# Turns by TensorE through one PSUM tile, a longer convolution lead, later units and loads of two blocks

## The chip, the cores and the metric

One core of one Trainium2 chip. The metric is device time in microseconds (us) of one execution; the kernel before and each variant were run alternately on the same chip, and fast runs are compared with fast runs (a single-core run over 1.5% above the fastest of its kernel counts as slow and is left out of the ratios). The runs e9 and e10 are from another chip than e1 to e8; each ratio is against the kernel before on the chip of the run.

## The reference, cut to what matters

```python
# x (8, 4224, 192); weight (8 heads, 7 taps); d_inner = 512
w = softmax(weight, axis=-1)
out = einsum('hk,bskhg->bshg', w, windows_of_7(x_padded))        # causal convolution
proj = out @ w_in; val, gate = proj[..., :512], proj[..., 512:]
for t in range(S):
    h = a[0, 0] * h + val[:, t, :]; ys[:, t, :] = h                # scan, from 0 in each sequence
result = (silu(gate) * ys) @ w_out
```

## The kernel before

The 33,792 rows of all sequences are cut into blocks of 960. Each engine has one part of the work: TensorE convolves, projects and multiplies by `w_out`; VectorE scans; ScalarE does SiLU and empties PSUM; GpSimd multiplies SiLU and scan and issues the loads of `x` (which cast to bf16). The order on every engine is the order in the program. Four words recur: a *pair* is one pass of the main loop (two steps), a *piece* half a block's convolution, a *turn* brings a convolved block into columns, and a *unit* is the last multiplication for 512 rows; the prediction begins with them in full. The parts that the change touches:

```python
    # P = 128, NC = 4, M = 120, BT = 8, BANK = 512, XG = 4; tiles of PSUM: 2 of values, 2 of all else
    xb_pool = ctx.enter_context(tc.tile_pool(name="xb", bufs=3))
    # ...
    ps_v = ctx.enter_context(tc.tile_pool(name="ps_v", bufs=2, space=bass.MemoryType.PSUM))
    ps_m = ctx.enter_context(tc.tile_pool(name="ps_m", bufs=2, space=bass.MemoryType.PSUM))

    def vtile():
        return ps_v.tile([P, 2 * BANK], FP32, name="pv")

    def mtile():
        return ps_m.tile([P, 2 * BANK], FP32, name="pm")

    def xtile(b):
        g, k = divmod(b, XG)
        if g not in xbs:
            xbs[g] = xb_pool.tile([K, XG * BT, D], BF16, name="xb")
        return xbs[g], FIRST[b] - FIRST[g * XG]

    def rows(a, n):
        return dataclasses.replace(
            xf, offset=(a * M - HB) * D, ap=[[D, K], [M * D, n], [1, D]]
        )

    def load_cast(b0, b1):
        xt, a0 = xtile(b0)
        n = sum(SIZES[b0:b1])
        if b1 == NSB:
            n -= 1
            e = HB + LAST
            nc.gpsimd.memset(xt[:, a0 + n, :], 0.0)
            nc.gpsimd.dma_start(xt[0:e, a0 + n, :], xf[T - e : T, :])
        nc.gpsimd.dma_start(xt[:, a0 : a0 + n, :], rows(FIRST[b0], n))
    # ...
    def turn_pe(b, engs):
        nh = SIZES[b] // 2
        y = ycs.pop(b)
        xc = xctile(b)
        w = half(b)
        for r in range(3):
            pool, name = (ps_v, "pv") if b == 0 and r == 2 else (ps_m, "pm")
            pt = pool.tile([P, 4 * BANK], BF16, name=name)
            for i in range(nh):
                nc.tensor.transpose(
                    pt[:, i * M : i * M + M],
                    y[0:M, (r * nh + i) * P : (r * nh + i + 1) * P], ident,
                )
            copy(
                engs[r], cols(xc, r * nh, nh),
                pt[:, 0:w].rearrange("p (t m) -> p t m", m=M),
            )
    # ... proj(), val(), gate(): 2 matmuls each, full (128 rows) or the rest (64 rows), into pv or pm
    def out_unit(u):
        ps = mtile()
        osb = o_pool.tile([P, UB, D], FP32, name="osb")
        first = None
        for k in range(2):
            mms = out_mm(ps, u, k, range(NC))
            if first is not None:
                apart(mms, [first], "another PSUM bank of the same tile")
            first = out_copy(nc.scalar, ps, osb, k)
        nc.sync.dma_start(o4[u], osb)

    BY_PE = (0, 1, 2, 3)

    def conv_piece(b, part):
        ps = mtile()
        conv_mm(ps, b, part)
        conv_evac([(nc.scalar, (0, 2))], ps, b, part)
        if part and b not in BY_PE:
            turn(b)
    # ...
    NP = NSTEP // 2
    LEAD = 6
    early = {0: (3, 4), 1: (4, 5), 2: (5, 6), 3: (6, 8), 6: (8, 10), 9: (10, 12)}
    for p in range(NP):
        s = 2 * p
        b = s // NC
        scan(s)
        if p:
            val(s + 1, True, True)
        gate(s, True, True)
        val(s + 1, False, False)
        gate(s, False, False)
        val(s + 2, False, True)
        gate(s + 1, False, True)
        silu(s)
        mul(nc.gpsimd, s)
        gate(s + 1, True, False)
        val(s + 2, True, False)
        silu(s + 1)
        if p < NP - 1:
            scan(s + 1)
            mul(nc.gpsimd, s + 1)
        if p in early:
            load_cast(*early[p])
        if p == 1:
            nc.gpsimd.dma_start(wout, moe_w_out.rearrange("(c p) m -> p c m", p=P))
        if s % NC == 0 and b >= 6 and b % XG == 2 and b + 6 < NSB:
            load_cast(b + 6, min(b + 6 + XG, NSB))
        late = 0 if b >= NSB - 7 else 2
        if LEAD <= p < NP - 2 and done_step(u) < s - late:
            units(1)
        if p == 0:
            turn_pe(1, [nc.scalar] * 3)
        if p in (2, 4):
            turn_pe(p // 2 + 1, [nc.scalar] * 3)
        for _ in range({0: 0, 1: 2, 4: 2, 13: 2}.get(p, 1)):
            if todo:
                b1, part = todo.pop(0)
                conv_piece(b1, part)
        if p == 0:
            nc.scalar.copy(xs, xsf)
        if p == 2:
            firsts()
        if p % 2 == 0 and p // 2 + 1 < NSB:
            patch(p // 2 + 1)
```

## Time and profile before

| kernel before | |
|---|---|
| time, median of the first 3 runs (lowest, highest) | 336.76 us (335.98, 337.2) |
| span in the profile | 335.6 us |
| busy: TensorE, VectorE, GpSimd, ScalarE | 95, 92, 92, 79% |
| first scan starts, last scan ends | 12.41 us, 327.91 us |
| two pairs in the steady middle | 8.74 us |

A pair holds two scans, and a scan can run only if TensorE has finished its values. So the start times of the scans are the kernel's clock: a delay of any engine that matters shows as a gap between two scans, and all later scans are late by it. Busy shares alone would not tell where the time goes, since three engines are nearly full. The views themselves stand in the prediction.

### The profile page before, as it was taken

The numbers are of one execution on the slowest core, as the hardware profiler recorded it, in microseconds if no ns is written. First come the engines' busy times: TensorE is split into PE (matmuls) and PEld (weight loads), VectorE is DVE, ScalarE is ACT, GpSimd is POOL, SyncE is SP. The second block draws the span as 40 slices with busy tenths as digits, with TensorE's granted clock in tenths as the row PEclk, the third lists the DMA queues.
The fourth block names the chain that finished last, engine by engine and source line by source line (L and its number), as shares of the span: only waits on it lengthen the run. The fifth ranks groups of instructions, "written<-read, shape, count | busy, mean of one in ns | idle before, by whom it ended". The sixth has DMA issues, their size and how long they took to land.

```text
span 335.6 us, 6814 instructions
## 1 busy us (share of the span) xinstructions
PE 319.6 (95%) x2581; PEld 191.1 (57%) x2581; DVE 309.9 (92%) x190; ACT 263.8 (79%) x454; POOL 308.7 (92%) x198
## 2 busy tenths in 40 slices
PE   8888799999999999999999999899999999999984
PEld 3443366565666665555666666465556566555554
DVE  2798899998999998999999999999999989999991
ACT  4587888788888887888888888788888878887663
POOL 5699999999998998899999999999999999989992
PEclk9999999999999999999999999999999999999999
DMA  7669979999996799559985999399978995444223
GB/s 173 71 65 121 109 133 200 158 218 169 215 192 177 116 187 255 159 97 173 222 227 108 176 190 237 96 142 212 255 143 108 135 293 144 140 132 131 96 93 144
DMA packets 100968, 53.80 MB, mean 160 GB/s; under 512 B 91371, under 2 KB 92423, under 8 KB 100935
## 3 DMA queue, kind: packets, MB, share of 16 engines
q1 hardware_dynamic: 59943, 39.32, 52.2%
q0 software_dynamic: 40448, 13.55, 37.6%
q10 hardware_dynamic: 544, 0.49, 0.5%
q8 instruction: 20, 0.33, 0.5%
q14 instruction: 13, 0.11, 0.1%
HBM read 28.46 MB, written 25.95 MB: 162 GB/s over the span
## 4 chain that ended last, share of the span: by engine, by line
PE 77%; DMA 8%; POOL 4%; DVE 3%; issue 3%; ACT 3%; DVEq 0%; ACTq 0%; POOLq 0%
PE pm L482 23%; PE pm L409 16%; PE pv L409 14%; PE pv L415 10%; DMA xc<-yc 8%; PE pm L415 6%; PE pm L253 5%; POOL y L473 3%; DVE h L450 3%; PE pm L193 2%; ACT sg L435 1%; POOL xb L128 1%; ACT yc L102 0%; ACT xc L102 0%; PE pm L367 0%
## 5 line engine op out<-in xcount | busy, mean ns | idle before, releaser
L473 POOL TENSOR_TENSOR y<-sg,h 128x960 bf16<-128x960 bf16 (+3 forms) x159 | 280.3, 1791 | 15.7 <-ACT sg L435 15.2
L450 DVE TENSOR_TENSOR_SCAN h<-av,h,pv 128x960 bf16<-128x960 f32 (+5 forms) x140 | 265.7, 1937 | 10.3 <-issue 2.7
L435 ACT ACTIVATE sg<-pm 128x960 bf16<-128x960 f32 (+2 forms) x144 | 135.6, 953 | 44.1 <-PE pm L415 34.7
L482 PEld LDWEIGHTS <-y 128*128 128x128 bf16 x1056 | 91.1, 114 | 12.8 <-issue 0.8
L482 PE MATMUL pm<-wout,y 128*128 128x192 bf16 x1056 | 97.6, 246 | 0.4 <-ACT sg L435 0.3
L409 PEld LDWEIGHTS <-w 128*128 128x128 bf16 x576 | 48.9, 97 | 61.2 <-issue 32.4
L409 PE MATMUL pv<-xc,w 128*128 128x480 bf16 (+2 forms) x288 | 80.7, 362 | 1.8 <-DVE h L450 1.5
L409 PE MATMUL pm<-xc,w 128*128 128x480 bf16 (+2 forms) x288 | 81.3, 364 | 0.7 <-ACT yc L102 0.6
L102 ACT COPY osb<-pm 128x384 f32<-128x384 f32 x131 | 62.7, 479 | 15.0 <-PE pm L482 12.9
L102 ACT CAST yc<-pm 128x256 bf16<-128x256 f32 (+2 forms) x140 | 59.7, 490 | 1.8 <-PE pm L253 1.6
L415 PE MATMUL pv<-xc,w 64*128 64x480 bf16 (+2 forms) x288 | 53.6, 365 | 5.4 <-DVE h L450 3.4
L415 PEld LDWEIGHTS <-w 64*128 64x128 bf16 x576 | 23.1, 94 | 53.8 <-issue 39.7
L415 PE MATMUL pm<-xc,w 64*128 64x480 bf16 (+2 forms) x288 | 52.7, 358 | 0.0
L450 DVE TENSOR_TENSOR_SCAN h<-av,pv 128x720 bf16<-128x720 f32 (+4 forms) x32 | 42.5, 1331 | 1.5 <-PE pv L415 1.5
L253 PE MATMUL pm<-xb,tb 126*128 126x192 bf16 (+1 forms) x280 | 34.1, 244 | 0.9 <-ACT xc L102 0.4
L253 PEld LDWEIGHTS <-tb 126*128 126x128 bf16 x288 | 24.7, 97 | 3.0 <-issue 1.7
L128 POOL DMA_DIRECT2D xb<-in_x_dram x14 | 20.5, 1464 | 0.1
L193 PE MATMUL pm<-wm 128*128 128x512 bf16 x24 | 8.6, 522 | 1.3 <-DVE wm L138 1.3
L193 PEld LDWEIGHTS <-wm 128*128 128x128 bf16 x24 | 2.8, 126 | 5.6 <-issue 3.9
L102 ACT COPY xc<-pm 128x480 bf16<-128x480 bf16 (+1 forms) x10 | 5.2, 549 | 0.4 <-PE pm L367 0.4
L367 PE MATMUL pm<-ident,yc 120*128 120x120 bf16 x42 | 3.8, 214 | 1.6 <-ACT sg L435 1.3
L367 PEld LDWEIGHTS <-yc 120*128 120x128 bf16 x45 | 2.9, 97 | 3.4 <-issue 2.2
(58 smaller groups left out, 27.4 us busy)
## 6 DMA issues: line engine op xcount, KB each, us to landing
out_dram<-osb SPq DMA_DIRECT2D x65, 384.0 KB
xb<-in_x_dram POOLq DMA_DIRECT2D x5, 1512.0 KB, 23.0
xb<-in_x_dram POOLq DMA_DIRECT2D x3, 756.0 KB, 10.2
xb<-in_x_dram POOLq DMA_DIRECT2D x5, 378.0 KB, 5.5
xb<-in_x_dram POOLq DMA_DIRECT2D x1, 1275.8 KB, 20.9
xc<-yc SPq DMA_TRANSPOSE x32
w1r<-in_moe_w_in_dram SPq DMA_DIRECT2D x1, 448.0 KB
xr<-in_x_dram ACTq DMA_DIRECT2D x1, 283.5 KB
```

Of the source, the lines that this page charges most:

```text
L102: return eng.copy(o, i) if eng is nc.scalar else eng.tensor_copy(o, i)
L128: nc.gpsimd.dma_start(xt[:, a0 : a0 + n, :], rows(FIRST[b0], n))
L193: nc.tensor.matmul(pw[:, 0:BANK], wm[:, 0:P], wm, start=True, stop=True)
L253: nc.tensor.matmul(pc[:, :, i * G : i * G + G], tb[:, h, :], xt[:, a0 : a0 + n, h * G : h * G + G], start=True, stop=True, skip_group_chec ...
L367: nc.tensor.transpose(pt[:, i * M : i * M + M], y[0:M, (r * nh + i) * P : (r * nh + i + 1) * P], ident,)
L409: nc.tensor.matmul(o, w1[:, m], cols(xc, k * nh, nh), start=start, stop=not start, skip_group_check=True,)
L415: nc.tensor.matmul(o, w2[r, m], cols(xc, 2 * nh, nh, r), start=start, stop=not start, skip_group_check=True,)
L435: nc.scalar.activation(sg[:, 0 : 2 * w], pgs.pop(s)[:, BANK - w : BANK + w], Act.Silu)
L450: nc.vector.tensor_tensor_scan(h[:, lo:hi], av[:, c : c + 1].to_broadcast([P, hi - lo]), pv[:, BANK - w + lo : BANK - w + hi], initial=0.0 ...
L473: eng.tensor_mul(yr[c][:, ring(t0 + lo, hi - lo)], sg[:, lo:hi], h[:, lo:hi])
L482: nc.tensor.matmul(ps[:, o : o + D], yr[c][:, r.start + j : r.stop : UB], wout[:, c, :], start=(c == 0 and j % 2 == 0), stop=(c == NC - 1) ...
```

## The change

Its intent: take the waits out of the first pairs (turns through one PSUM tile, block 4 turned by TensorE as well, the first unit one pair later, one more pair between a block's convolution and its use), and replace the bursts of four-block loads, behind which DMA transposes landed late, by loads of two blocks. In passing, the load of the output weights goes from pair 1 to pair 5, and small casts from ScalarE to GpSimd. Cut to its core:

```diff
-    XG = 4                                            # blocks per tile of x
+    XG = 2
-    xb_pool = ...(name="xb", bufs=3)
+    xb_pool = ...(name="xb", bufs=6)
 # turn_pe: for b > 0 one tile for all three groups, emptied by two copies (2/3 and 1/3)
-        for r in range(3):
-            pool, name = (ps_v, "pv") if b == 0 and r == 2 else (ps_m, "pm")
+        if b == 0:
+            groups = [(ps_m, "pm", (0,)), (ps_m, "pm", (1,)), (ps_v, "pv", (2,))]
+        else:
+            groups = [(ps_m, "pm", (0, 1, 2))]
 # ... (casts of xs and ysp moved to GpSimd)
-    BY_PE = (0, 1, 2, 3)
+    BY_PE = (0, 1, 2, 3, 4)
-    LEAD = 6
-    early = {0: (3, 4), 1: (4, 5), 2: (5, 6), 3: (6, 8), 6: (8, 10), 9: (10, 12)}
+    LEAD = 7
+    TURN = {2: 2, 4: 3, 5: 4}
+    early = {0: (3, 4), 1: (4, 5), 2: (5, 6), 3: (6, 7), 4: (7, 8)}
+    later = {2 * b1 - 9: (b1, b1 + 2) for b1 in range(8, NSB, 2)}
         mul(nc.gpsimd, s)
+        if p in later:
+            load_cast(*later[p])
         gate(s + 1, True, False)
-        if p == 1:
+        if p == 5:
             nc.gpsimd.dma_start(wout, ...)
-        if s % NC == 0 and b >= 6 and b % XG == 2 and b + 6 < NSB:
-            load_cast(b + 6, min(b + 6 + XG, NSB))
-        for _ in range({0: 0, 1: 2, 4: 2, 13: 2}.get(p, 1)):     # pieces per pair
+        for _ in range({0: 0, 1: 2, 3: 2, 6: 2}.get(p, 1)):
-        if p == 2:
+        if p == 3:
             firsts()
```

## The prediction

> **Words.** A block is 960 rows of the flattened sequence (8 groups of 120), worked off in four steps (one per 128 inner channels), so two loop passes ("pairs", p) per block. A unit is the last multiplication for 512 rows (16 matmuls, L482); a piece is half a block's convolution (4 matmuls, L253). A turn brings a convolved block into columns: by TensorE (L367, then copies), or by a DMA transpose.
>
> **What bounds the kernel now.** I began with the page's busy times and its chain.
>
> ```profile
> PE 319.6 (95%) x2581; PEld 191.1 (57%) x2581; DVE 309.9 (92%) x190; ACT 263.8 (79%) x454; POOL 308.7 (92%) x198
> ...
> PE 77%; DMA 8%; POOL 4%; DVE 3%; issue 3%; ACT 3%; DVEq 0%; ACTq 0%; POOLq 0%
> ```
>
> Three engines are above 92%, so little can be won: 2% is 6.7 us. The chain is TensorE's for 77%. To see the steady pace I read the timeline of TensorE in the middle, where one unit falls into each pair.
>
> ```profile
> 176.74 1.48 PE L482 MATMUL pm<-wout,y 128*128 128x192 bf16 x16
> ...
> 181.19 1.48 PE L482 MATMUL pm<-wout,y 128*128 128x192 bf16 x16
> ...
> 185.49 1.48 PE L482 MATMUL pm<-wout,y 128*128 128x192 bf16 x16
> ```
>
> Pairs take 4.45 and 4.30 us in turn, 8.74 for two (4.37 each). TensorE's own work is 4.30; two scans of VectorE, at a pitch of 2.13 to 2.17 us, are about as much. Both lock into this cycle through the PSUM tiles of the values. The change touches nothing in it: 65 pairs at 4.37 stay. What can be won is the time lost beside the cycle, and it shows as gaps of the scans, so the timeline of VectorE was next (in brackets the idle time before, and its releaser).
>
> ```profile
> 14.77 3.20 DVE L450 TENSOR_TENSOR_SCAN h<-av,pv 128x720 bf16<-128x720 f32 x2 [0.70 <-PE pv L415]
> 18.23 1.65 DVE L450 TENSOR_TENSOR_SCAN h<-av,pv 128x720 bf16<-128x720 f32 x1 [0.27 <-PE pv L415]
> ...
> 27.51 8.53 DVE L450 TENSOR_TENSOR_SCAN h<-av,h,pv 128x960 bf16<-128x960 f32 x4 [1.30 <-PE pv L415]
> 37.46 8.53 DVE L450 TENSOR_TENSOR_SCAN h<-av,h,pv 128x960 bf16<-128x960 f32 x4 [1.42 <-POOL y L473]
> ...
> 78.13 15.46 DVE L450 TENSOR_TENSOR_SCAN h<-av,h,pv 128x960 bf16<-128x960 f32 x8 [0.85 <-POOL y L473]
> ...
> 131.60 1.11 DVE L450 TENSOR_TENSOR_SCAN h<-av,h,pv 128x432 bf16<-128x432 f32 x1 [0.52 <-issue]
> ...
> 270.56 2.21 DVE L450 TENSOR_TENSOR_SCAN h<-av,h,pv 128x960 bf16<-128x960 f32 x1 [0.44 <-PE pv L409]
> 273.34 15.46 DVE L450 TENSOR_TENSOR_SCAN h<-av,h,pv 128x960 bf16<-128x960 f32 x8 [0.56 <-PE pv L415]
> ```
>
> The gaps of 1.30 and 1.42 follow the turns of blocks 2 and 3 (pairs 2 and 4); I do not believe the label POOL of the second, for the value matmuls that the scan needs end at 37.4. The 0.85 follows the doubled piece of pair 13. Those at 131 and 270 follow late DMA transposes, which the chain in order of time shows (start, length):
>
> ```profile
> 113.01 13.86 DMA xc<-yc
> ...
> 254.61 14.32 DMA xc<-yc
> ```
>
> and the page's DMA issues name the disturber (a load of four blocks in flight for 23 us):
>
> ```profile
> xb<-in_x_dram POOLq DMA_DIRECT2D x5, 1512.0 KB, 23.0
> xb<-in_x_dram POOLq DMA_DIRECT2D x3, 756.0 KB, 10.2
> xb<-in_x_dram POOLq DMA_DIRECT2D x5, 378.0 KB, 5.5
> ```
>
> By the landings in the trace a transpose takes 3.7 us with no load in flight, 7.4 (issued at 37.29) and 9.1 (at 63.63) inside a load of two blocks, and 11 to 14.3 inside one of four.
>
> **What the skill says.** "DMA: Bandwidth & Descriptors", Issuing engines are not separate DMA queues: DMAs of all issuing engines share the 16 DMA engines and interleave. The trace agrees: 3.7 us against 11 to 14. Same page, Anatomy of one DMA: about 2.0 us plus bytes over 436 GB/s. For 378 KB that gives 2.9 us; the trace has 5.5, so I take the trace. "TensorE: Matmul & The Clock Gate", Part 4: a transpose takes 275 to 390 ns alone. The trace has 214 ns, and four in a row take 0.37 us, a pitch of 52 ns. "PSUM — Partial Sum Buffer", the four PSUM rules: GpSimd can't reach PSUM; hence the new staging tile that ScalarE fills for GpSimd.
>
> **The change, part by part.**
>
> (1) Turns with one PSUM tile. Before, 12 transposes went through three tiles out of a pool of two, so TensorE waited for both SiLUs and then for the first copy:
>
> ```profile
> 23.38 0.38 PE L367 MATMUL pm<-ident,yc 120*128 120x120 bf16 x4
> 24.20 0.82 PE L367 MATMUL pm<-ident,yc 120*128 120x120 bf16 x8 [0.44 <-ACT sg L435]
> ```
>
> Now all 12 wait only for the first SiLU and take 12 x 0.052 = 0.6 us. ScalarE copies 960 and 480 columns (by the copies of 360 and 480, 0.46 and 0.56 us, some 0.96 + 0.51 = 1.47) in place of 3 in 1.58: nothing gained there. The next gate matmul still waits for both copies. I walked pairs 0 to 7 by hand with these lengths, in the program's order on each engine:
> - pair 0: turn of block 1; scan 3 no longer waits, at 17.96 in place of 18.23.
> - pair 2: copies end at 25.2, the gate matmuls 0.5 later, the value's second half 0.4 after; scan 7 at about 26.3 (27.51 before).
> - pair 3: two pieces and the small convolution of the sequences' first rows (moved here from pair 2), whose tile waits for the first piece's copies; scan 9 at 31.0 (31.74), a new gap of 0.4.
> - pair 4: turn of block 3; scan 11 at 35.5 (37.46).
> - pair 5: turn of block 4, new; scan 13 at 40.1 (41.69), a gap of 0.4.
> - pair 7: scan 15 at 44.4 (46.20), first unit of this pair at 45.85 (47.65).
> So the start gains 1.8 us. Block 4 adds 0.6 us of TensorE and 1.5 us of ScalarE, but in pair 5, which has no unit (1.32 us), so it is mostly hidden.
>
> (2) The lead. Blocks 6 to 8 get four pairs between convolution and use where they had three; the doubled piece goes from pair 13 (behind a unit) to pair 6 (none). The gap of 0.85 falls to the cycle's usual 0.13: 0.7 us won.
>
> (3) Units one pair later. By the loop's condition the old kernel skipped a unit in pair 44, the new one skips none; both reach 63 before the end. Pairs 44 and 45 took 8.73 us without that unit, the cycle as well: neutral. The tail keeps its three units (48 matmuls, 4.13 us).
>
> (4) Loads of two blocks, every four pairs. Two pairs' times at the late transposes were 9.71 and 9.80 us against 8.74: 2.0 us lost. A transpose has some 12.5 us until its patch or matmul. With 9 us it makes it: 2.0 us won. GpSimd pays 1.31 us for each of 14 such loads: per four pairs 8 products at a pitch of 1.97 (15.7) plus 1.3 is 17.1 of 17.5 us. It fits, and nothing waits for products that are late by 1.3 us (their tiles are double, the units lie several steps behind).
>
> (5) GpSimd takes over small casts (some 1 us together) and the load of the output weights goes from pair 1 to pair 5. Here I see a cost. GpSimd by my walk: products 8 and 9 end at 38.5, load of block 7 to 39.5, products 10 and 11 to 43.4, then the weights are issued. Their own landing time is not seen alone (5.6 us before, behind another load in the same queue); by the skill's formula an estimate of 2.5, by the trace's excess more, say 3 us: 46.4, against the first unit ready at 45.85. TensorE works in order, so I put 0.7 us of loss here.
>
> Sum: 1.8 - 0.7 + 0.7 + 2.0 = 3.8, and some 0.3 for small gaps of pairs 8 to 12 that came with TensorE's backlog: 4.1 us. 336.8 - 4.1 = 332.7.
>
> **Rivals.**
> (A) The weights land late, at 48 to 49, behind the load of block 7 and the transpose of block 5. Then the first unit waits 2 to 3 us and eats the start's whole gain: 334 to 335. For it speaks the 5.6 us of before, against it that the earlier load is then nearly done.
> (B) The smoother loads now meet a transpose every 17.5 us, and one deadline is still missed, or each disturbs the outputs: 334.5. Against it: no wait showed for those at 37 and 63 us.
> (C) The gaps of the start are only moved: the cycle is bound by TensorE, and its debt comes back; part 1 yields nothing: 334.
> (D) Without disturbances VectorE's floor rules (2.10 us a scan unhindered, 4.2 a pair) for many pairs: up to 0.1 us a pair, 330 or below. Against it: undisturbed stretches of 50 us before held 4.37.
>
> **Range and chances.** The rivals A to C cost 1.5 to 2 us each, two together give 335.5; all going well with something of D gives 330.3. Over 2% needs 330.0, twice the losses that I can name beyond the start: 0.07. Slower by 2% would need a new stall of 11 us: 0.01.
>
> **What would show it.** Scan gaps after turns below 0.5 us; the unit of pair 7 near 46; no wait of TensorE for the weights over 1 us; the transposes' landings at most 10 us and no wait on them; 4.37 us a pair between 100 and 300 us. I am wrong if the first unit waits for the weights, if the pair's pace changes, or if new gaps follow GpSimd's loads.

## The result

The changed kernel took 348.28 us in the median (347.52, 348.01 and 348.56 fast, one slow run of 355.09), the kernel before 336.37 in all its runs then. The ratio is 1.0351, interval 1.0301 to 1.0401. Ratios here are the mean time of one kernel's fast runs over that of the other's of the same rounds, so not quite the ratio of the medians quoted. So the change made the kernel 3.5% slower; 1.2% faster had been predicted.

The profiled run after (span 345.8 us), first its busy times and chain. Lines have moved: L254 is a piece (L253 before), L423 and L429 are the projections (L409, L415), L464 the scan (L450), L487 the product (L473) and L496 the unit (L482).

```profile
PE 322.5 (93%) x2593; PEld 193.0 (56%) x2593; DVE 309.9 (90%) x190; ACT 264.9 (77%) x449; POOL 314.4 (91%) x210
...
PE 59%; DMA 18%; POOL 10%; issue 8%; ACT 3%; DVE 1%; DVEq 0%; ACTq 0%; POOLq 0%
PE pm L496 16%; DMA xb<-in_x_dram 16%; PE pm L423 12%; PE pv L423 10%; POOL y L487 8%; PE pv L429 8%; PE pm L429 5%; PE pm L254 4%; PE pm L194 2%; ACT sg L449 2%; DMA wout<-in_moe_w_out_dram 1%; DVE h L464 1%; POOL xb L128 1%; DMA out_dram<-osb 1%; ACT xc L102 1%
```

VectorE is busy for the same 309.9 us: no work was added to it, it only waits more. The DMA share of the chain has gone from 8 to 18%, and it has new names: the loads of `x` and of `wout` (before, it was the transposes, `xc<-yc`). The list of waits after (in all, times, longest) says the same from TensorE's side:

```profile
PEld L254 <- DMA xb<-in_x_dram: 10.0, 9, 2.4
...
PE pm L254 <- DMA xb<-in_x_dram: 7.8, 7, 2.2
...
PE pm L496 <- DMA wout<-in_moe_w_out_dram: 2.6, 1, 2.6
```

(The weight load and the matmul behind it sit out the same wait; the two are not to be added. Of the seven waits of matmuls, one of 0.7 us at 24 us belongs to a load of the start, and most versions below have it too; six, 7.1 us in all, belong to the loads of two blocks.) In the kernel before, the waits for `xb` were

```profile
PEld L253 <- DMA xb<-in_x_dram: 0.2, 1, 0.2
```

Where it happened shows in the starts of the scans, read from the trace:

| scan (pair) | before, us | after, us | after minus before |
|---|---|---|---|
| 16 (8) | 48.33 | 45.94 | -2.39 |
| 20 (10) | 57.16 | 58.85 | +1.69 |
| 72 (36) | 173.17 | 177.16 | +3.99 |
| 100 (50) | 234.99 | 244.43 | +9.44 |
| 132 (66) | 306.07 | 316.21 | +10.14 |

The first scan itself started 0.35 us earlier after the change (12.06 us); from there to scan 16 the change won 2.04 us. So the start went as predicted. The timeline of VectorE after, with the gaps that answer to those of 0.27, 1.30 and 1.42 before:

```profile
25.89 4.32 DVE L464 TENSOR_TENSOR_SCAN h<-av,h,pv 128x960 bf16<-128x960 f32 x2 [0.40 <-PE pv L429]
30.52 4.32 DVE L464 TENSOR_TENSOR_SCAN h<-av,h,pv 128x960 bf16<-128x960 f32 x2 [0.31 <-POOL y L487]
35.06 4.32 DVE L464 TENSOR_TENSOR_SCAN h<-av,h,pv 128x960 bf16<-128x960 f32 x2 [0.22 <-issue]
39.60 7.83 DVE L464 TENSOR_TENSOR_SCAN h<-av,h,pv 128x960 bf16<-128x960 f32 x4 [0.22 <-issue]
```

Then 4.1 us are lost at once. The timeline of TensorE after, at the first unit:

```profile
44.90 0.57 PE L423 MATMUL pv<-xc,w 128*128 128x480 bf16 x2
48.03 2.72 PE L496 MATMUL pm<-wout,y 128*128 128x192 bf16 x16 [2.56 <-DMA wout<-in_moe_w_out_dram]
50.54 0.61 PE L254 MATMUL pm<-xb,tb 126*128 126x192 bf16 x4
```

The unit is ready at 45.3 (where e3, below, starts it), the weights land at 47.89, and then it takes 2.72 us where nearly all other units take 1.48. The windows over that stretch give the cause; the column after the five engines is the granted TensorE clock:

```profile
44.00:48.00 4.00, 1.47 (x8) 0.40 (x8) 4.00 (x3) 1.67 (x2) 4.00 (x3) 0.92 0.94 135
48.00:51.00 3.00, 2.97 (x21) 2.86 (x22) 0.17 (x1) 0.69 (x2) 2.98 (x3) 0.54 0.00 0
51.00:54.00 3.00, 3.00 (x23) 1.38 (x22) 1.62 (x2) 2.54 (x6) 2.38 (x2) 1.00 0.75 63
```

The clock's records show 0.5 from 47.37 for 3.41 us, and again from 231.69 for 3.41 us, after the longest wait for `xb`. That second stretch reads like this in the timeline of TensorE:

```profile
230.35 0.50 PE L254 MATMUL pm<-xb,tb 126*128 126x192 bf16 x4 [2.24 <-DMA xb<-in_x_dram]
...
233.27 0.98 PE L423 MATMUL pm<-xc,w 128*128 128x480 bf16 x2
234.05 1.01 PE L423 MATMUL pv<-xc,w 128*128 128x480 bf16 x2
```

Pairs of matmuls that take 0.57 us elsewhere take 1.0 here. From scan 88 to scan 99 the change took 28.09 us, and e2 (below), without late loads, 24.18: 3.9 us lost where the wait was 2.24, so the fall of the clock and what followed it cost up to 1.7 us. And the DMA issues after show why the loads are late:

```profile
xb<-in_x_dram POOLq DMA_DIRECT2D x13, 756.0 KB, 13.0
```

A load of two blocks took 10.2 us in the kernel before, 13.0 now (12.3 to 15.0 by the landings). It is issued in the middle of pair 2b-9 (b is the first of its blocks), and the piece that reads it comes at the end of pair 2b-6: three pairs of 4.37 us, 13.1 us. Lead and landing are about equal, so about half of the loads, six of thirteen, come late.

### The profile page after: what moved, and what is told of

It is laid out like the page before. It is cut to its first block, busy times and chain, and to the rows that moved or that the text cites. A ratio compares the mean times of both kernels' runs of the same rounds, so it can differ in the third digit from the quotient of the medians.

```text
span 345.8 us, 6840 instructions
## 1 busy us (share of the span) xinstructions
PE 322.5 (93%) x2593; PEld 193.0 (56%) x2593; DVE 309.9 (90%) x190; ACT 264.9 (77%) x449; POOL 314.4 (91%) x210
## 4 chain that ended last, share of the span: by engine, by line
PE 59%; DMA 18%; POOL 10%; issue 8%; ACT 3%; DVE 1%; DVEq 0%; ACTq 0%; POOLq 0%
PE pm L496 16%; DMA xb<-in_x_dram 16%; PE pm L423 12%; PE pv L423 10%; POOL y L487 8%; PE pv L429 8%; PE pm L429 5%; PE pm L254 4%; PE pm L194 2%; ACT sg L449 2%; DMA wout<-in_moe_w_out_dram 1%; DVE h L464 1%; POOL xb L128 1%; DMA out_dram<-osb 1%; ACT xc L102 1%
## 5 line engine op out<-in xcount | busy, mean ns | idle before, releaser
L487 POOL TENSOR_TENSOR y<-sg,h 128x960 bf16<-128x960 bf16 (+3 forms) x159 | 280.3, 1790 | 20.2 <-ACT sg L449 19.5
L464 DVE TENSOR_TENSOR_SCAN h<-av,h,pv 128x960 bf16<-128x960 f32 (+5 forms) x140 | 265.7, 1937 | 21.0 <-issue 12.4
L496 PE MATMUL pm<-wout,y 128*128 128x192 bf16 x1056 | 99.1, 248 | 4.2 <-DMA wout<-in_moe_w_out_dram 2.6
L496 PEld LDWEIGHTS <-y 128*128 128x128 bf16 x1056 | 92.1, 114 | 17.3 <-POOL y L487 4.5
L423 PEld LDWEIGHTS <-w 128*128 128x128 bf16 x576 | 49.1, 98 | 61.4 <-issue 32.9
L423 PE MATMUL pm<-xc,w 128*128 128x480 bf16 (+2 forms) x288 | 81.7, 366 | 1.6 <-ACT xc L102 1.1
L423 PE MATMUL pv<-xc,w 128*128 128x480 bf16 (+2 forms) x288 | 81.2, 364 | 0.6 <-DVE h L464 0.4
L429 PE MATMUL pv<-xc,w 64*128 64x480 bf16 (+2 forms) x288 | 53.9, 368 | 2.3 <-DVE h L464 1.7
L429 PE MATMUL pm<-xc,w 64*128 64x480 bf16 (+2 forms) x288 | 53.1, 362 | 0.0
L429 PEld LDWEIGHTS <-w 64*128 64x128 bf16 x576 | 23.5, 94 | 50.1 <-issue 38.8
L464 DVE TENSOR_TENSOR_SCAN h<-av,pv 128x720 bf16<-128x720 f32 (+4 forms) x32 | 42.4, 1329 | 1.2 <-PE pv L429 1.2
L254 PE MATMUL pm<-xb,tb 126*128 126x192 bf16 (+1 forms) x280 | 34.4, 245 | 8.8 <-DMA xb<-in_x_dram 7.8
L254 PEld LDWEIGHTS <-tb 126*128 126x128 bf16 x288 | 24.4, 98 | 12.2 <-DMA xb<-in_x_dram 10.0
L128 POOL DMA_DIRECT2D xb<-in_x_dram x21 | 25.5, 1214 | 0.1
L102 ACT COPY xc<-pm 128x960 bf16<-128x960 bf16 (+2 forms) x9 | 6.1, 728 | 0.6 <-PE pm L375 0.5
```

Source lines behind the costliest of these rows:

```text
L102: return eng.copy(o, i) if eng is nc.scalar else eng.tensor_copy(o, i)
L254: nc.tensor.matmul(pc[:, :, i * G : i * G + G], tb[:, h, :], xt[:, a0 : a0 + n, h * G : h * G + G], start=True, stop=True, skip_group_chec ...
L423: nc.tensor.matmul(o, w1[:, m], cols(xc, k * nh, nh), start=start, stop=not start, skip_group_check=True,)
L429: nc.tensor.matmul(o, w2[r, m], cols(xc, 2 * nh, nh, r), start=start, stop=not start, skip_group_check=True,)
L464: nc.vector.tensor_tensor_scan(h[:, lo:hi], av[:, c : c + 1].to_broadcast([P, hi - lo]), pv[:, BANK - w + lo : BANK - w + hi], initial=0.0 ...
L487: eng.tensor_mul(yr[c][:, ring(t0 + lo, hi - lo)], sg[:, lo:hi], h[:, lo:hi])
```

## The experiments

Two losses were on the table: the weights (4 us) and the loads (7 us and more). The rival causes were GpSimd's time in mid-pair, which would delay products, and the turn of block 4. Offsets of scans below are relative to the kernel before, with the first scans laid over each other.

**The weights alone.**

```diff
-        if p == 5:
+        if p == 1:
             nc.gpsimd.dma_start(wout, ...)
```

> The changed kernel with one thing undone: the output weights are loaded in pair 1, as before, not in pair 5. Theory: TensorE waited 2.56 us for them in the first unit, after which its granted clock stood at 0.5 for 3.4 us; scan 16 was 2.39 us ahead of the kernel before and scan 20 was 1.69 behind, so 4.1 us are lost there. Expected: 348.3 - 4 = 344 us, the first unit starting near 45.4 and no clock of 0.5 there. Rival (the start is slow because block 4 is turned by TensorE and its tiles, not because of the weights): less than 1 us won.

Measured: 344.33 us in the median of four runs, one slow (351.95) among them; ratio of the fast ones 1.0225 (1.0185 to 1.0265). The first unit took its usual time, with no clock below 1.0 there:

```profile
45.46 1.48 PE L496 MATMUL pm<-wout,y 128*128 128x192 bf16 x16
```

From scan 16 to scan 20 it took 8.87 us, and the change 12.91: 4.0 us. So the theory holds, and the rival, the turn of block 4, falls. Matmuls now waited 10.8 us for `xb`, 3.0 more than in the change's profile.

**The loads alone.**

```diff
-    later = {2 * b1 - 9: (b1, b1 + 2) for b1 in range(8, NSB, 2)}
+    later = {2 * b1 - 10: (b1, b1 + 2) for b1 in range(8, NSB, 2)}
```

> The changed kernel with the loads of two blocks issued one pair earlier, still in mid-pair, so GpSimd's work per pair is the same. Theory: the loads land 12.3 to 15 us after their issue, the first piece that needs them comes some 13 us after it, and seven late landings (7.8 us of waits of TensorE, plus one stretch of clock at 0.5) cost 7 us and more: expected 340 to 341 us and no wait of TensorE for a load. Rival (what costs is the 1.3 us of GpSimd in mid-pair, which delays the products): no change, 348.

Measured: 336.32 us, ratio 1.0008 (0.9971 to 1.0044): 11.5 us won by the ratios, more than expected. Waits of matmuls for `xb` fell from 7.8 to 0.6 us, and that one is the start's:

```profile
PE pm L254 <- DMA xb<-in_x_dram: 0.6, 1, 0.6
```

GpSimd's work was unchanged, so its time in mid-pair is not the cause. Landings fell too, to 8.2 to 10.4 us: here the next transpose was issued over 5 us behind the load, in the change 0.9 to 2.5 us behind. That is not the merit of even pairs as such, for in e3, in the same pairs, the first four loads had a transpose 2.5 to 3.9 us behind them and took 11.5 to 12.9 us, without harm. Two of the four runs took 337.3 us at a clock of 0.993, two 335.0 and 335.4 at 0.999: here the clock's fall came in some executions and not in others.

**Both.**

> Both of the above. If the two are all that went wrong and are independent: 348.3 - 4 - 7.5 = about 336.5; the start's lead of 2.4 us and the two removed transpose waits of 1.4 us together should then show as well, so 332.5 by the list of scans. Rival (there is a third cost, in turns or in the smoother loads): above 336.

Measured: 332.92 us, ratio 0.9902 (0.9881 to 0.9923). The two together explain the whole loss (the ratio won is 0.0449, the two alone won 0.0126 and 0.0343), and the time is then close to the 332.7 of the prediction, in part by luck, as shown below. The scans are 2.0 us ahead after the start and 3.8 us at pair 50. The waits of TensorE for DMA that are left:

```profile
PEld L254 <- DMA xb<-in_x_dram: 1.0, 2, 0.6
...
PE pm L254 <- DMA xb<-in_x_dram: 0.4, 1, 0.4
```

**Keeping TensorE busy while the weights are late.**

```diff
         first = None
+        if u == 0:
+            for _ in range(11):     # results overwritten by the unit
+                nc.tensor.matmul(ps[:, 0:BANK], wm[:, 0:P], wm, start=True, stop=True)
```

> The changed kernel with eleven idle matmuls of 512 columns (0.213 us each, 2.3 us in all) put ahead of the first unit, into its own tile, which the unit overwrites: TensorE is busy while it waits for the weights, which come as late as ever. Theory (half of what the late weights cost is the clock that falls to 0.5 after 2.6 us of idling): the unit takes 1.5 in place of 2.7 us and the kernel wins 1.3 to 1.8 us: 346.5 to 347. Rival (the clock drop costs nothing, since the unit was waiting anyway): 348.3 or more.

Measured: 345.88 us in the median of four, one slow (348.8) among them; ratio 1.0252 (1.0185 to 1.0319). The unit took 1.48 us, starting at 47.35 as the weights landed. But with this much scatter (341.67 to 345.94 in the fast runs), and a later wait of 3.7 us for a load that made the clock fall at 66.79 instead, the total proves little. So it was repeated without late loads.

> e2 (loads one pair earlier, weights as late as in the change) with the eleven idle matmuls ahead of the first unit. In e4 late loads blurred the effect; here there are none. e2 ran at 1.0008 of the kernel before, its first unit took 2.73 us, and the clock stood at 0.5 for 3.4 us. Theory (the fallen clock costs as much as half of it again, that is up to 1.7 us): the unit takes 1.48 us and the run is at 0.9955 to 0.997 of the kernel before, 334.6 to 335.1 us. Rival (the clock is beside the path): 1.0008.

Measured: 335.85 us, ratio 1.0004 (0.9989 to 1.0019), so the expected 0.9955 to 0.997 was missed. In the profile the theory holds. The timeline of TensorE in this run:

```profile
45.31 2.54 PE L516 MATMUL pm<-wm 128*128 128x512 bf16 x11
47.97 1.48 PE L496 MATMUL pm<-wout,y 128*128 128x192 bf16 x16
```

and of the run with the loads earlier and the weights late:

```profile
47.94 2.73 PE L496 MATMUL pm<-wout,y 128*128 128x192 bf16 x16 [2.35 <-DMA wout<-in_moe_w_out_dram]
```

Same landing, but scan 17 comes 1.35 us earlier. In the totals it is hidden because the clock had fallen in only two of that kernel's four runs. With the idle matmuls all six runs lay between 335.57 and 336.43 at a clock of 0.999 or more. So the fall costs 1.3 us at the first unit in the profile, about 2 us between the two kinds of runs (two against two), and the mean over runs does not show that this filler pays.

**Two pairs earlier.** (Against e3.)

```diff
-    later = {2 * b1 - 10: ...
+    later = {2 * b1 - 11: ...          # weights in pair 1, as in e3
```

> Weights in pair 1, loads two pairs earlier than in the change (again in odd pairs, so each meets a transpose issued some 2 us after it, as in the change), against one pair earlier in e3. Theory A (only the lead counts): loads land after 12 to 15 us, transposes after 10 to 11 us, both in time, so no wait: 333 us, the same as e3. Theory B (the phase against the transposes counts by itself): longer landings and waits for transposes, 335 or more.

Measured: 332.67 us, ratio 0.9894 (0.9871 to 0.9918), as e3. Back in odd pairs, most loads again took 12 to 15.6 us, and from 128 us on, where a transpose is again issued 0.75 to 1.05 us behind each load, nearly every other transpose took 10.3 to 12.2; with this lead it does no harm but for one transpose wait of 0.8 us near the start. In the change's phase both transfers are longer, but what costs time is the lead.

**The old loads.** e3 with tiles of four blocks in three buffers and the old load schedule.

> e3 with the old loads of x: four blocks at a time at a block's first pair, three tiles. It tells what the smaller loads are worth once they come in time. Theory: the loads of two blocks save the two late transposes of before, some 1.4 to 2.0 us by the scans, so this run is at 334.5 to 335. Rival (the gain over the kernel before is all in the start): 333.

Measured: 334.56 us, ratio 0.9953 (0.993 to 0.9977). Smaller loads in time are worth 1.6 us against e3. Not all of it is the transposes, for matmuls also waited 2.4 us for `xb` here; but late transposes are back in the list of waits, as in the kernel before:

```profile
ACT xc L334 <- DMA xc<-yc: 2.1, 2, 1.8
```

**Three tiles in the turns.** (Against e3.)

```diff
-            groups = [(ps_m, "pm", (0, 1, 2))]
+            groups = [(ps_m, "pm", (r,)) for r in range(3)]
```

> e3 with the turns of blocks 1 to 4 through three PSUM tiles again, everything else as in e3. Theory (the single tile takes away the waits for the second SiLU and for the first copy): the gaps of the scans after the turns come back, 0.3 us in pair 1, about 0.9 us in each of pairs 3, 5 and 6: 2 to 3 us slower, 335 to 336. Rival (the gain in the start comes from the units' later beginning and the moved pieces): within 0.5 us of e3.

Measured: 334.14 us, ratio 0.9946 (0.9929 to 0.9963): 1.2 us slower than e3, half of what was expected. Its gaps at scans 3, 7, 11 and 13 are 0.27, 0.67, 0.55 and 0.55 us; the single tile had none, then 0.40, 0.22 and 0.22 in the changed kernel's profile. The lead at scan 16 is 0.76 us with three tiles and 2.04 with one, so the single tile brings 1.3 us of the start's gain, the moved units, pieces and casts the rest.

**The last load.** In e3 and in the change one gap of GpSimd's making was left: the last load (a memset and two loads) stands in mid-pair just where the units come close behind the products. The timeline of TensorE in e3:

```profile
279.70 1.02 PE L496 MATMUL pm<-wout,y 128*128 128x192 bf16 x10 [0.87 <-POOL y L487]
```

> e3 with the last load (a memset and two loads, 2.1 us of GpSimd together) moved from pair 58 to pair 56. In e3 the only large gap left in the scans is 1.08 us at 282 us, where a unit waits for GpSimd's product, just after that load. Theory (GpSimd is behind by the load when the units come within two steps of the products): the gap goes, 1 us won, 331.9. Rival (the unit waits there anyway, for the steps' order): 332.9.

Measured: 332.51 us, ratio 0.9902 (0.9877 to 0.9927). The gap of the scans fell from 1.08 to 0.62 us, so one half of it went.

> e6 with the last load in pair 52 in place of 56. GpSimd gets back some 0.4 us per pair, so after 2.1 us of load it needs five pairs, and in e6 a gap of 0.62 us was left at the unit of pair 61. Theory: moved four pairs further the gap is gone, 0.5 us less than e6, about 332.0. Rival (the order of units and products makes that gap): as e6.

Measured: 332.12 us, ratio 0.9889 (0.9872 to 0.9906), the fastest version. It was run on another chip. In the profile the gap is gone: at scan 124 it is 0.9 us ahead of e3. TensorE then is 91% of the chain and DMA 1%. The gap's end is shown by the traces; between the totals of e3, e6 and e9 the intervals overlap. Its busy times and chain, over a span of 331.0 us:

```profile
PE 318.9 (96%) x2593; PEld 191.4 (58%) x2593; DVE 309.9 (94%) x190; ACT 264.6 (80%) x449; POOL 313.8 (95%) x210
...
PE 91%; ACT 5%; DVE 2%; DMA 1%; issue 1%; DVEq 0%; ACTq 0%
```

## Why the prediction was wrong

The prediction said 332.7 us, the kernel took 348.3. By its own steps:

1. *Turns and start: right.* "Scan gaps after turns below 0.5 us" came true (0.40, 0.31, 0.22, 0.22). The hand walk had scan 15 at 44.4, it was at 43.83, and the unit ready at 45.85, it was ready at 45.3. (Its two copies of ScalarE, 0.96 + 0.51, take 0.51 for the 480 columns that its own line puts at 0.56; together they took 1.42.)
2. *Lead: right.* The gap of 0.85 us at scan 29 fell to 0.13.
3. *Units later: no harm seen.* Pairs 44 and 45 took 8.83 us in the changed kernel, 8.74 before.
4. *Loads of two blocks: the step that failed.* The prediction asked whether the transposes would be in time ("With 9 us it makes it") and whether GpSimd had the 1.31 us, and both held: no wait for a transpose shows in the list after. But its sign for this, landings of at most 10 us, failed: every other transpose took 10.2 to 13.6. It never held the load's own landing against its own deadline. The two numbers were there: 10.2 us from the page, and three pairs, 13.1 us, from the schedule. Even so the margin would have looked like 3 us, because the 10.2 came from loads with few transposes beside them; in the new place the landing was 13.0. In place of "2.0 us won", the lag grew from 1.7 us at scan 28 to 9.4 at scan 100, with the clock's second fall among the causes. Rival B spoke of a missed deadline, but of a transpose's, at 1.5 to 2 us.
5. *The weights: right mechanism, wrong size.* "I put 0.7 us of loss here." The landing took 4.95 us, not "say 3", and 4.1 us were lost. Rival A had 48 to 49 us for the landing (it was 47.89) and a wait of 2 to 3 us (it was 2.56), but not the clock's fall, which put 1.3 us on top.
6. *A small one was missed:* "nothing waits for products that are late by 1.3 us". At the last load, with its 2.1 us, a unit did (1.3 us in the changed kernel's profile).

That e3, at 332.92, stands beside the predicted 332.7 is in part luck. Without the 0.7 us for the weights the parts add up to 4.8; e3 is 3.8 ahead by the scans and won 3.3 by the ratio. Start and lead held (2.0 and 0.7), what came between scans 29 and 116 was 1.7 in place of 2.3 (transposes and small gaps), the last load took 0.6 back, and the kernel before was itself 0.9 us faster in those runs. So most parts were sound, and two landings were set wrong: the loads' was not held against its deadline, the weights' was put too short. That both causes are what they are called is shown by e1, e2 and e3; that the clock's fall adds to a wait is shown in the profiles, and in the totals only by two runs against two.

## What to carry to other kernels

When a transfer is cut into smaller ones that are issued later, write down for each one issue, landing and first use, with the landing taken from the place where it will run, not from a quieter one; a lead that equals the landing gives late arrivals about half of the time. A load that is needed once, such as the output weights, cost nothing that shows here when it was issued early, and moving it late put it on the path. And a wait of TensorE of 2 us or more may cost more than its length, so it is the first to remove.

## What the Trainium skill lacked or had wrong

- "DMA: Bandwidth & Descriptors", Anatomy of one DMA: by its fit (2.0 us plus bytes over 436 GB/s) one estimates 2.5 us for the weights' 192 KB, 2.9 for 378 KB and 3.8 for 756 KB (bytes as written in bf16; by the fp32 bytes read 2.9, 3.8 and 5.6). Casting loads in this kernel took 4.75 to 5.65, 5.3 to 7.8, and 8.2 to 16.4 us. The fit has no term for other transfers in flight.
- "TensorE: Matmul & The Clock Gate", HAM oscillation: the rule given is no gap over some 3.4 us. Here gaps of 2.24, 2.35, 2.56 and 3.67 us were followed by a clock of 0.5, in e1's profile gaps of 2.14, 2.53 and 2.94 us were not, and one kernel fell in two runs of four. The same page's free-running window of 3413 ns (Part 1) agrees with the 3.41 us of each fall, and in every profile the changes of the clock lie whole windows apart (the two falls of the changed kernel 184.32 us, 54 windows). Laid on that grid, it is the idle time within one window that tells the cases apart: the four falls in mid-kernel came at the end of windows in which TensorE had idled for 1.91, 2.04, 2.08 and 2.25 us, while e1's gap of 2.94 us is cut into 1.08 and 1.85 and had no fall (nor had a window with 1.95 us at the very end of e8). So some 1.9 us in a window is an estimate of the limit, from these twelve profiles alone.
- The same page, Part 4: some 390 ns for a transpose of 128x128 in isolation, 275 in one kernel; here, for 120x120, 214 ns each, and four in a row in 0.37 us.
- No page says how much a DMA transpose and a load lengthen each other: the transpose took 3.7 us alone and 10.2 to 13.6 when issued 0.9 to 2.5 us after a load of two blocks; the load took 12.3 to 15.0 us then, and 8.2 to 10.4 in e2, where the transpose came over 5 us behind it.
